# Attention with a gated GLU on one core: the end of the last query chunk rearranged (gate rows kept in SBUF, last division in halves, output weight rows placed anew)

## The chip, the cores and the metric

The kernel runs on 1 core of one Trainium2 chip. The metric is device time in microseconds (us), the median of the runs; lower is better. One more execution was recorded by the hardware profiler; its rows are what is read here. Engines are called PE (matrix unit), PEld (its weight loads), DVE (vector), ACT (scalar), POOL (GpSimd) and SP (the queue that issues nearly all DMAs).

## The reference: what is computed

x is 2048 x 640, there are 32 heads of 20 columns, and the GLU is 1728 wide. Both branches read the same normalised rows.

```python
xn = layernorm(A_x)
q, k, v = split_heads(xn @ wqkv)            # 32 heads of 20
s = softmax(q @ k.T * 20 ** -0.5) @ v       # per head
s = merge_heads(s) @ wo                     # 640 x 640
h = sigmoid(xn @ w_gate) * (xn @ w_up)      # 2048 x 1728
g = silu(h @ w_down)                        # 2048 x 640
out = A_x + s * g
```

## The kernel before, in words

**Tiling.** The heads form 8 groups of 4 (`GH`), the queries 4 chunks of 512 (`QC`), and the keys 16 tiles of 128. A block is one group with one chunk: 32 blocks of 64 jobs, a job being one head against one key tile. The blocks of the last two groups alternate (`gc_of`, line 430), so the last two blocks are group 6 with chunk 3 and group 7 with chunk 3.

**The attention loop.** A job is a score matmul with a contraction of 32 rows (`score_mm`, line 829) into one of two PSUM pairs (`scA`) or one of three single banks (`bk`). ACT takes the exponential of two or three jobs at a time (line 80); DVE computes the exponential of other jobs by bit manipulation: a conversion to `iv` (line 1156) and three passes over four jobs (lines 915, 918, 921). The results, `pt` of ACT and `pb` of DVE, are multiplied with v on PE into the bank `oacc` (`pv_emit`, line 857): 20 rows and a row with the sum for each head.

**The division.** For 31 blocks, `norm_a` and `norm_b` (lines 878 to 908) copy `oacc` to SBUF, send the sums through DRAM and back to invert and broadcast them, multiply on POOL (line 897), and write the result with DMAs (line 905) into `oU`, whose 640 rows lie in 5 tiles of 128 partitions (`KD`). For the very last block the division is a chain of five steps between DVE and PE (`chain`, line 974): copy `oacc` (`e_on`, line 955), four transposes (`e_tr`, line 959), reciprocal and multiply (`div_scale`, lines 709 and 711), four transposes back (`e_back`, line 968), and a copy to a tile of its own, `o7` (`e_o`, line 972).

**The GLU.** Per chunk, gate and up tiles (line 647) give `hT`. Then eight down tiles (`mk_down`, line 677: 14 matmuls into 128 x 320, a tanh on ACT, one DVE operation on line 695) give the rows of g times 4, called `gqs`, which a DMA on SP writes to `gq_dram` (line 697).

**The output.** For chunks 0 to 2, `mk_out` (line 723) multiplies `oU` with `wo`. DVE multiplies with the g rows read back from `gq_dram` (line 742), POOL adds x (line 745), and a DMA stores. For chunk 3 the same is done by hand. `tail_load` (line 929) reads x rows and g rows from DRAM into the room of `wd`. `fill` (line 975) holds 40 matmuls, called fills below: for each of four query tiles, 5 over columns 0 to 511 (into `mains`, lines 940 and 946) and 5 over columns 512 to 639 (into `rest`, 128 wide). They cover the 560 rows that do not come from the last group; the fifth has 48 rows. `late_mm` (line 950) adds the 80 rows of the last group from `o7` with a copy of their weights, `wo_l`: 8 matmuls. `tail_steps` (line 980) ends the kernel: DVE multiplies `rest` (line 988) and adds x (line 993), multiplies each of the four `mains` (line 997), POOL adds x to three of them and DVE to the fourth (line 1000), and four DMAs store (line 1004).

**What sets the order.** PE, ACT and DVE run instructions in the order in which a planner in the kernel emits them (the loop from line 1067). It keeps a clock of its own with assumed durations, and at each step picks for PE a score group, a step of an item (`M`: output, down and other tiles), or a round of the product with v. When it finds nothing to do (`nxt is None`), it emits the next fill, if `can_fill` (line 1042) allows: all jobs claimed, no output or down tile in progress on PE, and for the banks also no items left and the bank free:

```python
if claimed[0] < NJOB * NBLK or cur is not None:
    return False
if f < 0:
    return slots[1]["a"] is None and slots[1]["ends"] <= now
return not items and all(it.bank != f for it in active if it.i < len(it.ops)) and flex[f] <= now
```

The first entry of a fill is `f`: below 0 for the two `mains` in `scA[1]`, 0 and 1 for those in banks 0 and 1, 2 for `rest`. `tail_steps` is emitted when the chain and all fills are out. SP's DMAs stay in the order of emission.

Of the kernel before, what the change touches and what calls it, by code (L numbers as in the profile page):

```python
# [18 lines left out]
P = 128  # L19
# [14 lines left out]

LOG2E = 1.4426950408889634
# [14 lines left out]
def kernel(  # L50
# [625 lines left out]

    def mk_down(c, t4, h, at):
        st = {}
        tt = 4 * c + t4

        def alloc():
            st["ps"] = misc_ps()

        def mm(kf):
            nc.tensor.matmul(st["ps"][:, 0:HD], lhsT=hT[0:fsz[kf], kf, t4 * P:(t4 + 1) * P],  # L685
                             rhs=wd[0:fsz[kf], kf, h * HD:(h + 1) * HD],
                             start=(kf == 0), stop=(kf == NFT - 1))

        def th():
            st["td"] = w2.tile([P, HD], BF16, tag="td", bufs=2, name="td")  # L690
            act_imm(st["td"], st["ps"][:, 0:HD], ACT.Tanh, 0.25)

        def ev():
            gqs = w2.tile([P, HD], FP32, tag="gqs", bufs=3, name="gqs")
            nc.vector.scalar_tensor_tensor(out=gqs, in0=st["td"], scalar=1.0, in1=st["ps"][:, 0:HD],
                                           op0=ALU.add, op1=ALU.mult)
            nc.sync.dma_start(out=gq_dram[tt * P:(tt + 1) * P, h * HD:(h + 1) * HD], in_=gqs)
        return Item([("PE", alloc, [(0.14, lambda kf=kf: mm(kf)) for kf in range(NFT)]),
                     ("ACT", 0.32, th), ("DVE", 0.40, ev, "free", mark("d", c, t4, h))], at, pre=[("h", c, kf) for kf in range(NFT)])


    FL = (NG - 1) * GC
    t_l, o_l = divmod(FL, P)
    wo_l = late.tile([GC, D], BF16, name="wo_l")

    def div_scale(tps):
        tpv = tps.rearrange("p (i j r) -> p i j r", i=4, r=32)
        rq = w2.tile([P, 4, GH, 1], FP32, tag="rt", bufs=2, name="rq")
        nc.vector.reciprocal(out=rq, in_=tpv[:, :, :, 0:1])
        onq = w2.tile([P, 4, GC], BF16, tag="on_bf", bufs=2, name="onq")  # L710
        nc.vector.tensor_tensor(out=onq.rearrange("p i (j e) -> p i j e", e=DH), in0=tpv[:, :, :, 1:1 + DH],
                                in1=rq.broadcast_to((P, 4, GH, DH)), op=ALU.mult)
        return onq
# [173 lines left out]
    def norm_b(b, on, lt):  # L887
# [10 lines left out]
        for j in range(GH):  # L898
            f = g * GC + j * DH
            r = 32 * j + 1  # L900
            left = DH
            while left:
                t, o = divmod(f, P)
                m = min(left, P - o)
                nc.sync.dma_start(out=oU[o:o + m, t, c * QC:(c + 1) * QC], in_=on_bf[r:r + m, :])
                f += m
                r += m
                left -= m
# [15 lines left out]
    wfl = wd.rearrange("p k s -> p (k s)")  # L924
    hfl = hT.rearrange("p k s -> p (k s)")
    EX = D - 512
    tail = []

    def tail_load():
        for t4 in range(4):  # L930
            r = slice(4 * (NQC - 1) * P + t4 * P, 4 * (NQC - 1) * P + (t4 + 1) * P)
            o2 = wfl[:, t4 * 3 * D:(t4 + 1) * 3 * D]
            tail.append((o2[:, 0:D], o2[:, D:3 * D].bitcast(FP32)))
            nc.sync.dma_start(out=tail[t4][0], in_=x2[r, :])
            nc.sync.dma_start(out=tail[t4][1], in_=gq_dram[r, :])


# [6 lines left out]
    def early(dst, t4, sl, kd, start=True):  # L944
        rows = P if kd < t_l else o_l
        nc.tensor.matmul(dst, lhsT=oU[0:rows, kd, c0 + t4 * P:c0 + (t4 + 1) * P], rhs=wo[0:rows, kd, sl],
                         start=(start and kd == 0), stop=False, skip_group_check=True)

    def late_mm(dst, t4, sl):
        nc.tensor.matmul(dst, lhsT=last["o"][:, t4 * P:(t4 + 1) * P], rhs=wo_l[:, sl], start=False, stop=True,  # L950
                         skip_group_check=True)

    def e_on():
        last["on"] = w2.tile([P, QC], FP32, tag="on", bufs=2, name="on")
        nc.vector.tensor_copy(out=last["on"], in_=oacc)

    def e_tr():
        for i in range(4):
            nc.tensor.transpose(out=scA[0][:, 0, i * P:(i + 1) * P], in_=last["on"][:, i * P:(i + 1) * P],
                                identity=ident_f)  # L960

    def e_scale():
        last["q"] = div_scale(scA[0][:, 0, :])

    def e_back():
        last["t"] = psum.tile([P, 2 * QC], BF16, name="tp2", tag="oacc")
        for i in range(4):
            nc.tensor.transpose(out=last["t"][0:GC, i * P:(i + 1) * P], in_=last["q"][:, i, :], identity=ident)

    def e_o():  # L970
        last["o"] = w2.tile([GC, QC], BF16, tag="rl", bufs=1, name="o7")
        nc.vector.tensor_copy(out=last["o"], in_=last["t"][0:GC, 0:QC])

    chain = [("DVE", 0.60, e_on), ("PE", 1.52, e_tr), ("DVE", 0.75, e_scale), ("PE", 0.42, e_back), ("DVE", 0.45, e_o)]
    fill = [(t4 - 2, 0.2133, lambda t4=t4, kd=kd: early(mains[t4], t4, slice(0, 512), kd))
            for t4 in range(4) for kd in range(t_l + 1)]
    fill += [(2, 0.07, lambda t4=t4, kd=kd: early(rest[:, t4 * EX:(t4 + 1) * EX], t4, slice(512, D), kd, t4 == 0))
             for t4 in range(4) for kd in range(t_l + 1)]

    def tail_steps():  # L980
        for t4 in range(4):
            late_mm(rest[:, t4 * EX:(t4 + 1) * EX], t4, slice(512, D))
        for t4 in range(4):
            late_mm(mains[t4], t4, slice(0, 512))
        tmps = [hfl[:, t4 * 2 * D:t4 * 2 * D + 1024].bitcast(FP32) for t4 in range(4)]
        xg = wfl[:, 0:12 * D].rearrange("p (t u) -> p t u", u=3 * D)
        tmp = hfl[:, 8 * D:8 * D + 8 * EX].bitcast(FP32)
        nc.vector.scalar_tensor_tensor(out=tmp.rearrange("p (t e) -> p t e", e=EX),
                                       in0=rest.rearrange("p (t e) -> p t e", e=EX), scalar=0.25,
                                       in1=wfl[:, 0:12 * D].bitcast(FP32).rearrange(  # L990
                                           "p (t u) -> p t u", u=3 * D // 2)[:, :, D // 2 + 512:3 * D // 2],
                                       op0=ALU.mult, op1=ALU.mult)
        nc.vector.tensor_tensor(out=xg[:, :, 512:D], in0=tmp.rearrange("p (t e) -> p t e", e=EX),
                                in1=xg[:, :, 512:D], op=ALU.add)
        for t4 in range(4):
            xr, gqr = tail[t4]
            nc.vector.scalar_tensor_tensor(out=tmps[t4], in0=mains[t4], scalar=0.25, in1=gqr[:, 0:512],
                                           op0=ALU.mult, op1=ALU.mult)
            add = nc.vector if t4 == 3 else nc.gpsimd
            add.tensor_tensor(out=xr[:, 0:512], in0=tmps[t4], in1=xr[:, 0:512], op=ALU.add)  # L1000
        for t4 in range(4):
            r = slice(4 * (NQC - 1) * P + t4 * P, 4 * (NQC - 1) * P + (t4 + 1) * P)
            eng = nc.sync if t4 % 2 == 0 else nc.scalar
            eng.dma_start(out=out2[r, :], in_=tail[t4][0])

    with tc.manual_schedule(engines={ENG.PE, ENG.Activation, ENG.DVE}):
        nc.sync.dma_start(out=wo, in_=A_wo.rearrange("(kd p) e -> p kd e", p=P))
        nc.sync.dma_start(out=wo_l, in_=A_wo[FL:D, :])
# [33 lines left out]
        def can_fill(f):  # L1042
            if claimed[0] < NJOB * NBLK or cur is not None:
                return False
            if f < 0:
                return slots[1]["a"] is None and slots[1]["ends"] <= now
            return not items and all(it.bank != f for it in active if it.i < len(it.ops)) and flex[f] <= now
# [16 lines left out]

        guard = 0
        chain_at = 1e9
        while chain or fill or items or glu_items or any(it.i < len(it.ops) for it in active):
# [11 lines left out]
            if not tail and not glu_items and q_at.get(NBLK - 1, 1e9) <= now and not any(  # L1079
                    it.need is None for it in items + active):  # L1080
# [20 lines left out]
            for eng in ("ACT", "DVE"):  # L1101
                if free[eng] > now:
                    continue
                if chain and chain[0][0] == eng and chain_at <= now:
                    _, dur, f = chain.pop(0)
                    f()
                    free[eng] = now + dur
                    chain_at = now + dur + EL
# [80 lines left out]
            if free["PE"] <= now and chain and chain[0][0] == "PE" and chain_at <= now:  # L1189
                _, dur, f = chain.pop(0)  # L1190
                f()
                free["PE"] = now + dur
                chain_at = now + dur + PL
                mode = "M"
            if free["PE"] <= now:
# [107 lines left out]
                elif nxt is None and fill and can_fill(fill[0][0]):  # L1303
                    free["PE"] = now + fill[0][1] + (T_MODE if mode != "M" else 0.0)
                    fill.pop(0)[2]()
# [47 lines left out]
```

## Time and profile before

| what | value |
|---|---|
| median of 3 runs | 838.99 us (837.27 to 840.88) |
| the profiled execution's own time | 838.14 us |
| its span, first to last instruction | 836.4 us |
| busy: PE, DVE, ACT, POOL | 782.4, 751.7, 798.5, 83.2 us |
| mean granted PE clock | 0.991 |
| PE busy in 807 to 812, and in 812 to 816 | 4.91 of 5.00 us, 3.99 of 4.00 us |
| ACT's last instruction ends | 817.1 us |

How to read it: an instruction row of the timeline gives the start in us from the span's start, the time covered in us, engine, line, operation, output and inputs with shapes, and a count when neighbours are merged; in brackets the idle time before it and what released it. A matmul's row lasts from its start to the end of its result, and the next one starts before that, so the distance between starts is what PE spends on one. The chain of waits gives start, duration and what the time went to, followed back from the last instruction.

### The profile page before, as it was taken

The page shows a single profiled execution, that of the slowest core. Times are in us where ns is not written, and L with a number is a line of the kernel's source. Part 1 is how long each engine was busy: PE and PEld are TensorE (multiplying, and loading weights), DVE is VectorE, ACT ScalarE, POOL GpSimd, SP SyncE. Part 2 cuts the span into 40 slices and gives each one's busy share as a digit, 9 for nine tenths or more (in the row PEclk, how much of TensorE's full clock was granted, in tenths as well). Part 3 has the DMA queues.
Part 4 walks back from the last instruction along what each step waited for, and adds up shares of the span by engine and source line. Part 5 has one row for each costly group of instructions (what it writes and reads, how often), then busy time and mean ns, then how long its engine had stood idle before and what let it go on. Part 6 is the DMA issues. An engine that isn't in the chain of part 4 may idle for free.

```text
span 836.4 us, 16903 instructions
## 1 busy us (share of the span) xinstructions
PE 782.4 (94%) x6330; PEld 276.5 (33%) x6389; DVE 751.7 (90%) x1178; ACT 798.5 (95%) x1000; POOL 83.2 (10%) x90
## 2 busy tenths in 40 slices
PE   4899999999999999999999999999999999999995
PEld 2432223333333323333333323333333223333332
DVE  7689998998899999888999988999889999989994
ACT  7699999999999999999999999999999999999990
POOL 5000000000000000000000000000000003104041
PEclk9899999999999999999999999999999999999998
DMA  5612312122221232212122233221311223314124
GB/s 155 195 31 60 76 43 52 52 61 73 71 68 51 61 85 61 73 50 78 42 62 63 68 84 78 63 83 53 93 46 58 82 81 98 93 46 137 50 72 144
DMA packets 93587, 62.58 MB, mean 75 GB/s; under 512 B 35044, under 2 KB 86884, under 8 KB 93504
## 3 DMA queue, kind: packets, MB, share of 16 engines
q1 hardware_dynamic: 93216, 61.16, 26.0%
q8 instruction: 50, 0.82, 0.4%
q10 hardware_dynamic: 288, 0.33, 0.1%
q14 instruction: 33, 0.27, 0.1%
HBM read 46.51 MB, written 12.40 MB: 70 GB/s over the span
## 4 chain that ended last, share of the span: by engine, by line
ACT 49%; PE 29%; DVE 11%; issue 7%; DMA 2%; SPq 1%; POOLq 0%; POOL 0%; ACTq 0%; DVEq 0%
ACT pt L80 45%; PE scA L830 9%; PE oacc L867 6%; PE bk L685 4%; DVE iv L1156 4%; PE bk L647 4%; ACT tnh L80 2%; DVE pb L921 2%; PE bk L510 2%; DVE pb L915 1%; DVE pb L918 1%; PE bk L735 1%; PE bk L618 1%; PE psk L140 1%; DMA lt<-ld 1%
## 5 line engine op out<-in xcount | busy, mean ns | idle before, releaser
L80 ACT ACTIVATE pt<-scA 128x1024 bf16<-128x1024 f32 x734 | 722.1, 1147 | 5.7 <-PE bk L830 1.9
L1156 DVE TENSOR_SCALAR iv<-bk 128x512 int16<-128x512 f32 x465 | 315.8, 683 | 45.7 <-PE bk L830 44.5
L830 PE MATMUL scA<-q,kT 32*128 32x512 bf16 x1462 | 285.8, 384 | 17.9 <-ACT pt L80 10.5
L830 PE MATMUL bk<-q,kT 32*128 32x512 bf16 x586 | 211.7, 386 | 1.4 <-DVE iv L1156 1.2
L867 PE MATMUL oacc<-pt,v 128*21 128x512 bf16 x1583 | 182.6, 382 | 0.3 <-issue 0.3
L830 PEld LDWEIGHTS <-kT 32*128 32x128 bf16 x2048 | 88.4, 91 | 267.3 <-issue 253.8
L867 PE MATMUL oacc<-pb,v 128*21 128x512 bf16 x930 | 150.6, 382 | 1.0 <-DVE pb L915 0.4
L921 DVE TENSOR_TENSOR pb<-iv,pb 128x2048 bf16<-128x2048 bf16 (+1 forms) x117 | 145.6, 1245 | 0.7
L647 PE MATMUL bk<-xnT,wgu 128*128 128x512 bf16 x475 | 140.5, 383 | 4.6 <-issue 1.9
L897 POOL TENSOR_TENSOR on_bf<-on,rl 128x512 bf16<-128x512 f32 x31 | 42.1, 1358 | 677.4 <-DMA rl<-rd 452.5
L80 ACT ACTIVATE pt<-bk 128x512 bf16<-128x512 f32 x121 | 86.7, 717 | 4.2 <-DVE oacc L388 2.8
L685 PE MATMUL bk<-wd,hT 128*128 128x320 bf16 x448 | 87.1, 302 | 2.2 <-DVE iv L1156 1.5
L915 DVE TENSOR_SCALAR pb<-iv 128x2048 int16<-128x2048 int16 (+1 forms) x117 | 84.5, 722 | 2.7
L918 DVE TENSOR_SCALAR pb<-iv 128x2048 int16<-128x2048 int16 (+1 forms) x117 | 83.4, 713 | 0.0
L867 PEld LDWEIGHTS <-v 128*21 128x21 bf16 x2513 | 49.2, 91 | 85.2 <-issue 62.9
L647 PEld LDWEIGHTS <-wgu 128*128 128x128 bf16 x520 | 37.4, 97 | 65.5 <-issue 47.2
L510 PE MATMUL bk<-xnT,wu 128*120 128x512 bf16 x160 | 50.0, 400 | 0.1
L685 PEld LDWEIGHTS <-hT 128*128 128x128 bf16 x448 | 34.4, 97 | 46.2 <-issue 37.0
L80 ACT ACTIVATE tnh<-bk 128x512 bf16<-128x512 f32 (+1 forms) x56 | 41.5, 742 | 0.1
L655 DVE SCALAR_TENSOR_TENSOR hT<-tnh,bk 128x512 bf16<-128x512 bf16 x52 | 35.3, 680 | 4.3 <-PE bk L647 2.9
L618 PE MATMUL bk<-wv,xnT 128*128 128x160 bf16 x280 | 31.6, 243 | 1.1 <-DVE v L189 0.5
L745 POOL TENSOR_TENSOR xnT<-otmp,xnT 128x320 bf16<-128x320 f32 x24 | 24.2, 1011 | 45.7 <-DVE otmp L742 45.5
(105 smaller groups left out, 366.8 us busy)
## 6 DMA issues: line engine op xcount, KB each, us to landing
rl<-rd SPq DMA_DIRECT2D x124, 64.0 KB
wgu<-in_B_w_gate_dram SPq DMA_DIRECT2D x24, 320.0 KB
wgu<-in_B_w_up_dram SPq DMA_DIRECT2D x24, 320.0 KB
gq_dram<-gqs SPq DMA_DIRECT2D x32, 160.0 KB
xnT<-gq_dram SPq DMA_DIRECT2D x12, 320.0 KB
xt<-in_A_x_dram SPq DMA_DIRECT2D x16, 160.0 KB
oU<-on_bf SPq DMA_DIRECT2D x108, 20.0 KB
wd<-in_B_w_down_dram SPq DMA_DIRECT2D x1, 2080.0 KB
```

Source lines behind the costliest of these rows:

```text
L80: return nc.scalar.add_instruction(mybir.InstActivation(func=func, name=nc.get_next_instruction_name(), engine=ENG.Activation, ins=[nc.sca ...
L510: nc.tensor.matmul(st["ps"][0:UC, :], lhsT=wus[u][:, kd, i, :], rhs=xnT[:, c, kd, :], start=(kd == 0), stop=(kd == KD - 1))
L618: nc.tensor.matmul(st["ps"][:, i * 2 * GC:(i + 1) * 2 * GC], lhsT=xn_tok(tts[i], kd), rhs=wvs[pr][:, kd, :], start=(kd == 0), stop=(kd == ...
L647: nc.tensor.matmul(st[key][0:fs, :], lhsT=w[:, i, kd, ko * P:ko * P + fs], rhs=xnT[:, c, kd, :], start=(kd == 0), stop=(kd == KD - 1))
L685: nc.tensor.matmul(st["ps"][:, 0:HD], lhsT=hT[0:fsz[kf], kf, t4 * P:(t4 + 1) * P], rhs=wd[0:fsz[kf], kf, h * HD:(h + 1) * HD], start=(kf = ...
L830: nc.tensor.matmul(dst, lhsT=kTs[gc_of(b)[0] % 2][32 * j:32 * j + 32, kt * P:(kt + 1) * P], rhs=qts[b % 3][32 * j:32 * j + 32, :], start=T ...
L867: nc.tensor.matmul(oacc[32 * j:32 * j + DH + 1, :], lhsT=lhsT, rhs=u["src"], start=first, stop=last, tile_position=(0, 32 * j), skip_group ...
L897: nc.gpsimd.tensor_tensor(out=on_bf, in0=on, in1=rl, op=ALU.mult)
L915: nc.vector.tensor_scalar(out=pb[:, 0, :, :].bitcast(I16), in0=iv, scalar1=0x7F80, scalar2=1, op0=ALU.bitwise_and, op1=ALU.bitwise_or)
L918: nc.vector.tensor_scalar(out=pb[:, 1, :, :].bitcast(I16), in0=iv, scalar1=0x007F, scalar2=0x3F00, op0=ALU.bitwise_and, op1=ALU.bitwise_or)
L921: nc.vector.tensor_tensor(out=pb[:, 1, :, :], in0=iv.bitcast(BF16), in1=pb[:, 1, :, :], op=ALU.mult)
L1156: nc.vector.tensor_scalar(out=d["iv"][:, j, :], in0=bank[bk], scalar1=B_OFF, scalar2=0.0, op0=ALU.add, op1=ALU.max)
```

## The change: what it does

1. **Gate rows of chunk 3 stay in SBUF.** Line 695's result goes into a tile of the pool `wgu` (`gq_last`, two query tiles each, float32) in place of `gqs`. The 8 writes to `gq_dram` and the 4 reads of chunk 3 are gone. The x rows of chunk 3 are loaded into the room of `xnT`'s chunk 3, as soon as the last `hT` tile of chunk 3 is computed.
2. **Rows of `oU` and `wo` in the last of the five tiles change place.** The last group's 80 rows come first (partitions 0 to 79), the 48 rows before them come after (80 to 127). The fills then run over four full tiles, 32 in place of 40, and each late matmul over the whole fifth tile, 128 rows in place of 80. `wo_l` is gone, and `e_o` writes into `oU`.
3. **The last division runs in two halves of 256 queries.** Each of the five steps becomes two, with dependencies written out; the two scale steps wait for both transposes.
4. **Fills in another order, under another condition.** First the `mains` in banks 0 and 1 (query tiles 2 and 3), then `rest`, then the `mains` in `scA[1]`. Those for banks may start when 24 jobs are unclaimed (`FILL_AT`). A bank with a fill in it is closed to others.
5. **`tail_steps` by halves.** Late matmuls: `mains` 0 and 1, `rest` 0 and 1, then 2 and 3 likewise. DVE: the multiply of `mains` 0 and 1, then `rest` of these two (256 wide), the same for 2 and 3, and the addition for `mains` 3 at the end.

The diff, cut to its core:

```diff
+FILL_AT = 24
+    def gq_last(t4):
+        if len(gq_l) == t4 // 2:
+            w = w2.tile([P, 2, KD, 2 * P], BF16, tag="wgu", bufs=2, name="gql")
+            gq_l.append(w.rearrange("p i k f -> p (i k f)").bitcast(FP32))
+        return gq_l[t4 // 2][:, t4 % 2 * D:(t4 % 2 + 1) * D]
...
         def ev():
+            if c == NQC - 1:
+                nc.vector.scalar_tensor_tensor(out=gq_last(t4)[:, h * HD:(h + 1) * HD], in0=st["td"], scalar=1.0,
+                                               in1=st["ps"][:, 0:HD], op0=ALU.add, op1=ALU.mult)
+                return
...
+                if t == KD - 1:
+                    o = f - FL if f >= FL else f - FK + D - FL
                 nc.sync.dma_start(out=oU[o:o + m, t, c * QC:(c + 1) * QC], in_=on_bf[r:r + m, :])
...
-            nc.sync.dma_start(out=tail[t4][0], in_=x2[r, :])
-            nc.sync.dma_start(out=tail[t4][1], in_=gq_dram[r, :])
+            tail.append(xl[:, t4 * D:(t4 + 1) * D])
+            nc.sync.dma_start(out=tail[t4], in_=x2[r, :])
...
-        nc.tensor.matmul(dst, lhsT=last["o"][:, t4 * P:(t4 + 1) * P], rhs=wo_l[:, sl], start=False, stop=True,
-                         skip_group_check=True)
+        nc.tensor.matmul(dst, lhsT=oU[:, KD - 1, c0 + t4 * P:c0 + (t4 + 1) * P], rhs=wo[:, KD - 1, sl], start=False,
+                         stop=True, skip_group_check=True)
...
-    chain = [("DVE", 0.60, e_on), ("PE", 1.52, e_tr), ("DVE", 0.75, e_scale), ("PE", 0.42, e_back), ("DVE", 0.45, e_o)]
+    chain = [("DVE", 0.34, lambda: e_on(0), ()), ("DVE", 0.34, lambda: e_on(1), ()),
+             ("PE", 0.40, lambda: e_tr(0), (0,)), ("PE", 0.40, lambda: e_tr(1), (1,)),
+             ("DVE", 0.50, lambda: e_scale(0), (2, 3)), ("DVE", 0.50, lambda: e_scale(1), (2, 3)),
+             ("PE", 0.25, lambda: e_back(0), (4,)), ("PE", 0.25, lambda: e_back(1), (4, 5)),
+             ("DVE", 0.27, lambda: e_o(0), (6,)), ("DVE", 0.27, lambda: e_o(1), (7,))]
...
-            for t4 in range(4) for kd in range(t_l + 1)]
+            for t4 in (2, 3, 0, 1) for kd in range(KD - 1)]
+    fill[2 * (KD - 1):2 * (KD - 1)] = [
+        (2, 0.07, lambda t4=t4, kd=kd: early(rest[:, t4 * EX:(t4 + 1) * EX], t4, slice(512, D), kd, t4 == 0))
+        for t4 in range(4) for kd in range(KD - 1)]
...
+        for i in range(2):
+            for t4 in (2 * i, 2 * i + 1):
+                late_mm(mains[t4], t4, slice(0, 512))
+            for t4 in (2 * i, 2 * i + 1):
+                late_mm(rest[:, t4 * EX:(t4 + 1) * EX], t4, slice(512, D))
+        for i in range(2):
+            for t4 in (2 * i, 2 * i + 1):
+                nc.vector.scalar_tensor_tensor(out=tmps[t4], in0=mains[t4], scalar=0.25, in1=gq_last(t4)[:, 0:512],
+                                               op0=ALU.mult, op1=ALU.mult)
+                if t4 < 3:
+                    nc.gpsimd.tensor_tensor(out=tail[t4][:, 0:512], in0=tmps[t4], in1=tail[t4][:, 0:512], op=ALU.add)
+            nc.vector.scalar_tensor_tensor(out=tmp[:, 2 * i:2 * i + 2, :],
...
+            nc.vector.tensor_tensor(out=xg[:, 2 * i:2 * i + 2, 512:D], in0=tmp[:, 2 * i:2 * i + 2, :],
+                                    in1=xg[:, 2 * i:2 * i + 2, 512:D], op=ALU.add)
+        nc.vector.tensor_tensor(out=tail[3][:, 0:512], in0=tmps[3], in1=tail[3][:, 0:512], op=ALU.add)
...
+        nc.sync.dma_start(out=wo[:, 0:KD - 1, :], in_=A_wo[0:FK, :].rearrange("(kd p) e -> p kd e", p=P))
+        nc.sync.dma_start(out=wo[0:GC, KD - 1, :], in_=A_wo[FL:D, :])
+        nc.sync.dma_start(out=wo[GC:P, KD - 1, :], in_=A_wo[FK:FL, :])
...
         def can_fill(f):
-            if claimed[0] < NJOB * NBLK or cur is not None:
+            if cur is not None or NJOB * NBLK - claimed[0] > (FILL_AT if f >= 0 else 0):
                 return False
             if f < 0:
                 return slots[1]["a"] is None and slots[1]["ends"] <= now
+            if f in filled:
+                return True
...
-            if not tail and not glu_items and q_at.get(NBLK - 1, 1e9) <= now and not any(
-                    it.need is None for it in items + active):
+            if not tail and all(ev_at.get(("h", NQC - 1, kf), 1e9) <= now for kf in range(NFT)):
                 tail_load()
...
                 elif nxt is None and fill and can_fill(fill[0][0]):
                     free["PE"] = now + fill[0][1] + (T_MODE if mode != "M" else 0.0)
+                    if fill[0][0] >= 0:
+                        filled.add(fill[0][0])
+                        flex[fill[0][0]] = 1e9
                     fill.pop(0)[2]()
```

## The prediction

> **What bounds the kernel now.** I read the page first. ACT, PE and DVE are all near full until the last slice, so no stage before the end has spare time, and the change touches only the end.
>
> ```profile
> PE   4899999999999999999999999999999999999995
> DVE  7689998998899999888999988999889999989994
> ACT  7699999999999999999999999999999999999990
> ```
>
> Then the chain of waits over the last 17 us, which says what the end hangs on:
>
> ```profile
> 818.29 1.19 PE scA L946 x4
> ...
> 820.11 4.44 DMA gq_dram<-gqs
> ...
> 824.62 2.72 DMA wd<-gq_dram
> ...
> 827.41 0.70 DVE hT L988
> ...
> 831.97 1.56 POOLq L1348
> ```
>
> The last gate tile goes to DRAM (4.44 us) and comes back (2.72 us); only then, at 827.41, does DVE start the tail. That looks like 7 us to be had. The chain names only the last arrival, though, so I looked at what came just before it, in PE's timeline:
>
> ```profile
> 817.37 0.59 PE L946 MATMUL scA<-wo,oU 128*128 128x512 bf16 x2 [0.16 <-issue]
> 817.90 0.39 PE L867 MATMUL oacc<-pt,v 128*21 128x512 bf16 x1
> ...
> 818.22 1.25 PE L946 MATMUL scA<-wo,oU 128*128 128x512 bf16 x4
> 819.40 0.39 PE L867 MATMUL oacc<-pb,v 128*21 128x512 bf16 x1
> 819.72 0.93 PE L946 MATMUL scA<-wo,oU 128*128 128x512 bf16 x3
> ...
> 822.74 0.39 PE L968 MATMUL tp<-ident,onq 128*80 128x128 bf16 x4
> 822.96 2.87 PE L946 MATMUL bk<-wo,oU 128*128 128x512 bf16 x23
> 825.76 0.40 PE L950 MATMUL bk<-wo_l,o 80*128 80x128 bf16 x4
> 826.00 0.59 PE L950 MATMUL scA<-wo_l,o 80*128 80x512 bf16 x2
> 826.43 0.59 PE L950 MATMUL bk<-wo_l,o 80*128 80x512 bf16 x2
> ```
>
> PE works on fills (L946) without a gap until 825.76, and its late matmuls end at 827.02, only 0.39 us before DVE starts. The division's last copy ended at 823.64, so neither the division nor the DMA holds PE: the fills do. The DMA pair hides a PE queue nearly as long as itself. Last, DVE and POOL:
>
> ```profile
> 817.20 0.49 DVE L695 SCALAR_TENSOR_TENSOR gqs<-td,bk 128x320 f32<-128x320 bf16 x1 [0.56 <-ACT td L80]
> 828.14 0.69 DVE L993 TENSOR_TENSOR wd<-hT,wd 128x512 bf16<-128x512 f32 x1
> 829.71 3.83 POOL L1000 TENSOR_TENSOR wd<-hT,wd 128x512 bf16<-128x512 f32 x3 [16.48 <-DVE hT L997]
> 831.46 1.07 DVE L1000 TENSOR_TENSOR wd<-hT,wd 128x512 bf16<-128x512 f32 x1
> ```
>
> POOL's third addition ends at 833.54; its store and the closing take 2.86 us more, to 836.4. I keep these 2.86 us: the last store remains one of the same size.
>
> **The change, step by step.** All times are of the profiled execution.
>
> *Early fills (FILL_AT): 0.* A fill needs an empty list of items and no tile in progress on PE. The last output tile starts at 809.05, and from there PE goes from row to row (3.99 of 4.00 us busy from 812 to 816) until the last down tile ends at 815.78, after all scores are out. There is no idle step for the planner to give away, so I expect the order up to 817 unchanged. The bounds are below, as rivals.
>
> *Fills before the last v product: 0.45 us gained.* Before, seven fills stand ahead of it (one record of them is missing). Following the planner's rules, the last down tile lies in bank 0, and now the first fill is for bank 0, so it waits until line 695 has read that bank: 817.69, some 0.09 later on PE. That is a new wait; behind it in PE's queue stand the other fills and the last v product. The three fills of 817.1 to 817.9 fall out, the pair of v products moves ahead of them, and I count five fills before the last product becomes ready for the planner: 817.78 + 5 x 0.213 (819.72 to 820.57 is four) = 818.85, and with the 0.1 that a switch costs (818.22 to 819.40 holds four fills and more) the product starts at 818.95 in place of 819.40. It can't start before 818.03, when `pb` is done.
>
> *PE from there to the late matmuls: 6.04 becomes 5.2 us.* Before, from 819.72 to 825.76: 13 fills of 512 columns x 0.213 = 2.77, 20 narrow ones at 0.108 (822.96 to 825.76 less 3 x 0.213, over 20) = 2.16, the transposes 0.65 (820.59 to 821.24) and 0.22, idle 0.24. After: 32 fills less 5 leave 11 x 0.213 = 2.35 and 16 x 0.108 = 1.73; the transposes keep 0.87; for two more handovers between DVE and PE I add 0.25. So from 819.27 to 824.47.
>
> *The halves of the division: hidden.* Half a copy of `oacc` has no row; it lies between 0.34 (half of 0.69) and 0.69. From 0.49 for 320 columns and 0.69 for 512 I take 0.42. Then 819.37 + 2 x 0.42 = 820.21 for the copies, 820.9 for the second transposes, two scale halves of 0.6 each (0.26 and 0.49 halved in their variable part) 822.0, back and copied by 823.0. PE has fills to 824.47, so the division is covered by 1.5 us; without that cover its own length would count.
>
> *DVE's start: 2.46 us earlier.* Now wide late matmuls come first. First result 0.39 after its start and 0.09 for switch and semaphore: 824.95 in place of 827.41.
>
> *DVE's tail: 0.5 us shorter.* Before, 6.13 us from 827.41 to POOL's end. After, DVE does four multiplies of 0.65 (828.94 to 830.24 for two) = 2.60, two half multiplies of 0.42 = 0.84, two half additions, and one addition of 512. An addition of this form took 0.69 alone (L993) and 1.07 beside POOL (L1000), a factor of 1.55. The halves run beside POOL: 2 x 0.42 x 1.55 = 1.30 (bounds 0.84 and, each waiting for a whole POOL addition of 1.28, 3.4). The last runs as POOL ends: 0.69. Gaps 0.2. Sum 5.63. POOL, fed from 0.65 on, needs 3.83 and ends at about 4.6, ahead of DVE. So the end is 824.95 + 5.63 + 2.86 = 833.44 in place of 836.4: 2.96 us gained.
>
> The Trainium skill's "SBUF — State Buffer", section "Who interferes with whom", says that a DVE operation with two SBUF inputs and a GpSimd operation that reads SBUF share a port as an exclusive lock, the later one blocked for the whole instruction. The row differs: 1.07 us beside POOL is 0.38 more than alone, far less than the 0.8 then left of POOL's addition (its second ended near 832.26). By the rule the two half additions would lose some 0.5 us more, and the end would be 833.9.
>
> *At nothing:* the gate result written into SBUF under another name (0.49 either way; the `wgu` buffers had their last reader before the last `hT` row at 733.43, so there is no wait); one more weight DMA at the start, hidden behind 800 us of other work (bounds 0 and 0.7, an issue of line 905); eight writes and four reads less on SP, which in the last 40 us waited mostly for POOL and DVE. The x loads now fall to about 734.1, right behind that `hT` row: four issues of 0.37 on SP, and behind them the inverted sums of a division, sent at 735.15 before. They may go 0.5 later; POOL waits for them for microseconds anyway, and only an output tile much later reads the result (bounds 0 and 0.9).
>
> *Sum:* -2.96. The profiled execution took 838.14, so 835.2; the median of the runs lies 0.85 above it, and I put the forecast on the median: 838.99 - 2.96 = **836.0**, that is 0.35% faster. A measurement of this kernel can tell about 0.5%, or 4.2 us, from no change, so the likeliest reading is "the same".
>
> **Rivals.**
>
> *Forecast (0.66): PE's fills stay the last to arrive.* Own range -2.2 to -3.8: port bounds of DVE's additions (-0.5 to +0.8) and 0.3 either way on PE; 834.9 to 836.8 before scatter.
>
> *Fills really go early (0.13).* If the planner finds idle steps for some 15 fills before the last product, PE is done when the division is. The product then starts at 818.1, 0.85 sooner; the division takes 3.65 from there on (823.0 less 819.37), so late matmuls start near 822.2 in place of 824.47. That is 2.3 more: -5.2, 833.8. For it: the division had been ready 2.1 us before PE. Against: PE shows no gap to put them in.
>
> *The split costs PE what the fewer fills save (0.13).* A handover from DVE to PE showed 0.29 (820.51 to 820.80) and 0.5 (822.22 to 822.74). If each of the four new ones stops PE by that because no fill is placed between, PE loses 1.2 to 2.0 in place of 0.25; the DMA's removal then uncovers PE at once and gains little: -1.3 to -2.0, about 837.3. For it: PE's order is fixed by assumed durations.
>
> *Slower (0.08): the early fill blocks PE.* One of bank 0's four fills reads the tile of `oU` that the second of five DMAs of line 905 completes. Those start at 812.51, 0.7 apart; issue to use took 1.67 beyond the last issue for line 895's, so that tile is there at 815.5. Should the four come out right after 809.05's tile, PE stands from about 810.9 to 815.5: 4.6 us in which DVE and ACT run dry, with 1 us to refill. -2.96 + 5.6 = +2.6: 841.6. It decides against the change from a stall of 3 us on, and as measurably slower from 7 us. For it: nothing in the condition looks at that DMA. Against: the same lack of idle steps.
>
> **How the numbers follow.** The three runs spread over 3.6 us, so a difference of medians carries about 1.5 us. Of the forecast's 0.66 some 0.13 then falls beyond -4.2, with most of 0.13 from early fills: faster 0.25. Slower by over 4.2: 0.03. Within: 0.72. The range takes in the forecast with its scatter, the third case, and the near part of the second: 833.9 to 838.3.
>
> **What would show it.** Right: the chain's end without a DMA link before DVE; PE's fills up to about 824.5 and DVE's first multiply near 825.0; PE's rows before 817 in the same order; five fills before the last v product; the last addition on DVE near 830.5. Wrong: fills before 815; idle time of PE between 819 and 824.5; DVE's start before 824 or after 826; half additions of over 0.9 us.

## The result

| | before | changed |
|---|---|---|
| median | 838.99 us (836.02 to 842.81, 7 runs) | 832.09 us (831.65 to 834.81, 7 runs) |
| profiled execution, span | 836.4 us | 829.9 us |
| mean granted PE clock in it | 0.991 | 0.997 |
| the last score group (line 830, now 842): start of its third matmul | 814.51 | 811.98 |
| from there to the end of the span | 21.91 us | 17.92 us |

The ratio is 0.9926, interval 0.9898 to 0.9953: faster by 6.9 us, where 3.0 were forecast. Twelve later runs gave a ratio of 0.995 (0.9924 to 0.9975): 833.54 against 837.6, 4.1 us. The last two rows of the table say why the two differ: 3.99 us of the 6.5 us between the profiles lie at the end, where the change is, and 2.5 us were there before the first instruction that it moves.

The page of the changed kernel, by slices, is that of before to within a tenth up to the last slice:

```profile
PE   4799999999999999999999999999999999999996
...
DVE  7789998998899999888999988999989998989996
ACT  7799999999999999999999999999999999999992
...
PEclk9999999999999999999999999999999999999998
```

In the last slice PE has 6 where it had 5, DVE 6 for 4 and ACT 2 for 0. The row of the clock has a 9 in its second place, where before had an 8: a small digit, to which experiment 6 comes back.

Its chain of waits no longer holds a DMA. It runs over PE's fills (now line 955), the transposes of the division, and DVE:

```profile
816.38 0.32 PE oacc L879
816.70 0.75 PE bk L955 x3
...
818.27 0.34 DVE onq L723
...
819.54 1.73 PE scA L955 x8
821.26 0.45 PE scA L959 x2
821.71 0.02 issue
821.73 1.29 DVE hT L1018 x2
```

PE's timeline, to be compared with the one in the prediction (its times lie about 2.5 us lower throughout):

```profile
815.14 1.24 PE L955 MATMUL bk<-wo,oU 128*128 128x512 bf16 x5 [0.24 <-DVE gql L704]
816.31 0.39 PE L879 MATMUL oacc<-pb,v 128*21 128x512 bf16 x1
816.63 0.82 PE L955 MATMUL bk<-wo,oU 128*128 128x512 bf16 x3
...
817.82 0.78 PE L955 MATMUL bk<-wo,oU 128*128 128x128 bf16 x11
818.65 0.31 PE L980 MATMUL tp<-ident,onq 128*80 128x128 bf16 x2
...
821.10 0.59 PE L959 MATMUL scA<-wo,oU 128*128 128x512 bf16 x2
```

Five fills stand ahead of the last v product, as forecast, and the first waits for line 704 (695 before). But eleven narrow fills take 0.62 us, counted from start to start (817.82 to 818.44, 0.056 each), not the 1.19 that 0.108 each would make; and the late matmuls come 4.47 us after the fill that follows that product (816.63 to 821.10), not 5.2. DVE and POOL:

```profile
821.73 1.29 DVE L1018 SCALAR_TENSOR_TENSOR hT<-scA,gql 128x512 f32<-128x512 f32 x2 [1.98 <-PE scA L959]
...
823.39 0.61 DVE L1026 TENSOR_TENSOR xnT<-hT,xnT 128x256 bf16<-128x256 f32 x1
...
825.57 0.84 DVE L1026 TENSOR_TENSOR xnT<-hT,xnT 128x256 bf16<-128x256 f32 x1
826.33 0.68 DVE L1028 TENSOR_TENSOR xnT<-hT,xnT 128x512 bf16<-128x512 f32 x1
822.57 3.56 POOL L1021 TENSOR_TENSOR xnT<-hT,xnT 128x512 bf16<-128x512 f32 x3 [11.89 <-DVE hT L1018]
```

DVE ends last, at 827.01, and 2.89 us later the span ends: the 2.86 of before.

### The profile page after: what moved, and what is told of

It reads as the page before. It is cut to its first block, busy times and chain, and to the rows that moved or that the text cites. A ratio compares the mean times of both kernels' runs of the same rounds, so it can differ in the third digit from the quotient of the medians.

```text
span 829.9 us, 16926 instructions
## 1 busy us (share of the span) xinstructions
PE 785.7 (95%) x6381; PEld 274.5 (33%) x6381; DVE 752.2 (91%) x1184; ACT 798.1 (96%) x1000; POOL 82.9 (10%) x90
## 5 line engine op out<-in xcount | busy, mean ns | idle before, releaser
L648 PE MATMUL bk<-xnT,wgu 128*128 128x512 bf16 x520 | 149.3, 383 | 2.6 <-DVE iv L1185 1.2
L694 PEld LDWEIGHTS <-hT 128*128 128x128 bf16 x448 | 34.4, 97 | 45.2 <-issue 35.9
L81 ACT ACTIVATE tnh<-bk 128x512 bf16<-128x512 f32 (+1 forms) x56 | 40.9, 731 | 0.1
```

Source lines behind the costliest of these rows:

```text
L81: return nc.scalar.add_instruction(mybir.InstActivation(func=func, name=nc.get_next_instruction_name(), engine=ENG.Activation, ins=[nc.sca ...
L648: nc.tensor.matmul(st[key][0:fs, :], lhsT=w[:, i, kd, ko * P:ko * P + fs], rhs=xnT[:, c, kd, :], start=(kd == 0), stop=(kd == KD - 1))
```

## The experiments

Because 2.5 us came from elsewhere, each kernel is read twice: its median beside the kernel before on the same chip, and, in its profile, the time from the last score group to the end of the span, called its **end** here and counted from the start of that group's third matmul. The end is steady: 17.92, 17.85, 17.88 and 17.91 us in four executions of the changed end. (Counted from the group's first matmul, a_order has 17.39 in place of 17.20; elsewhere the two differ by 0.06 at most.)

| kernel | median (before, same chip) | ratio, interval | end |
|---|---|---|---|
| before | 837.6 to 838.2 on three chips | | 21.91 |
| gate rows only (e_gate) | 835.37 (837.9) | 0.9976, 0.9957 to 0.9995 | 20.65 |
| rows placed only (e_rows) | 838.65 (837.9) | 0.9998, 0.9979 to 1.0018 | 22.68 |
| both of these (e_both) | 833.04 (837.6) | 0.9944, 0.9923 to 0.9965 | 17.80 |
| both, new tail order (e_mix) | 833.42 (837.6) | 0.9956, 0.9936 to 0.9975 | 17.32 |
| whole change (after_again) | 833.54 (837.6) | 0.995, 0.9924 to 0.9975 | 17.85 |
| change, old fill order (a_order) | 832.22 (837.79) | 0.9941, 0.9918 to 0.9963 | 17.20 |
| change, 48-row fills (a_rows48) | 835.54 (837.9) | 0.9968, 0.995 to 0.9986 | 20.34 |
| the same, filled up to 128 (a_rows128) | 833.9 (837.9) | 0.9951, 0.9936 to 0.9967 | 18.77 |

**1. Gate rows alone.** Edit: the new branch in `ev` of `mk_down`, `gq_last`, and `tail_load` with x only; all else as before.

> The kernel before with the gate rows of the last chunk kept in SBUF and nothing else changed (the narrow multiply of the tail in two pieces, since the rows lie in two tiles). Theory A (PE's queue of fills ends only 0.4 us before the DMA pair it was hidden behind): DVE's tail starts when the first late matmuls are done, 1.2 us sooner than before; the time falls by 1.0 to 1.5 us, 0.15%. Rival B (the DMA pair was the bound): it falls by 4 us or more, most of what the whole change brings at its end.

The end fell by 1.26 us, as A says, with the DMA pair gone entirely. (The median fell by 2.5 us, more than forecast; the interval of its ratio leaves room for 0.4 to 3.6.) Its chain of waits shows what stood behind the pair:

```profile
821.65 2.70 PE bk L957 x23
824.35 0.34 PE bk L961 x4
824.70 0.02 issue
824.72 0.77 DVE hT L1000 x2
```

PE's fills run straight up to the late matmuls, and DVE starts as the first of these end. Rival B is ruled out.

**2. Rows placed alone.** Edit: the new offset in `norm_b`, the split load of `wo`, fills over four full tiles, late matmuls over the fifth.

> The kernel before with the rows of oU and wo placed anew and nothing else: 32 fills over full tiles, late matmuls over 128 rows; the gate rows still go through DRAM. Theory A: PE's late matmuls start 2 us or more sooner, but DVE still waits for the DMA pair at the same place; time unchanged within 0.5 us. Rival B: PE's saving shows in the time, 2 us or more faster.

Late matmuls started 8.50 us after the last score group in place of 11.25, and none of it reached the time. The chain:

```profile
819.77 5.05 DMA gq_dram<-gqs
...
824.90 2.81 DMA wd<-gq_dram
...
827.88 0.70 DVE hT L986
```

DVE waits for the DMA pair as before; this time the write took 5.05 us where the profiled execution of before had 4.44, and the end is 0.8 later for that. So each of the two parts hides the other.

**3. Both together.**

> The kernel before with parts 1 and 2 only (gate rows in SBUF, rows placed anew); division in one piece, fills in the old order and under the old condition, old order of the tail. From the profiles of the two single steps: the first late matmul 8.5 us after the last score group (with the rows alone), 0.43 to DVE's start, 8.96 from there to the end (with the gate rows alone): 17.9 us, as much as the whole change has (17.92). Theory G (the two parts bring all of it together, and neither alone, since each uncovers the other): the same time as the changed kernel within 0.5 us. Rival H (the halves and the new order carry a good part): 1 us or more slower than the changed kernel.

> Parts 1, 2 and 5: as the kernel with parts 1 and 2, with the changed kernel's order of the tail by halves (wide late matmuls first). Theory G: first late matmul at 8.5 us after the last score group, DVE 0.63 later, 8.17 from there to the end as in the changed kernel: 17.3 us, 0.6 us faster than the changed kernel. Rival H: the division in halves is needed for the early start; 17.9 us or more.

Theory G holds for the end: 17.80 with the two parts, 17.32 with the new order of the tail as well, so the changed kernel's other parts (halves, order of fills) cost about 0.6 us. The median with the new order shows no gain over the whole change (833.42 and 833.54, where 0.6 was expected); eleven of its twelve runs had a mean clock of 0.994 or less, a matter of experiment 6.

**4. Which of them costs it.** Edit: `for t4 in range(4)` in `fill`, the narrow ones at the end, as before; halves kept.

> The changed kernel with the old order of the fills (those into the pair scA first, then banks 0 and 1, the narrow ones last); division in halves as in the changed kernel. Theory I (the new order makes PE wait 0.42 us for line 704 to read bank 0, and puts the cheap narrow fills under the division, so PE also waits 0.36 us there): the first late matmul comes 8.5 to 8.7 us after the last score group in place of 9.1, the time is 0.5 us shorter. Rival J (the order is right, the halves cost it): 9.1 or later.

The first late matmul came at 8.42 us, the end at 17.20. It is the order, not the halves: the changed kernel's PE waits 0.42 us for bank 0 (814.72 to 815.14; some 0.1 of it any switch from a v product to a fill costs, see experiment 5) and twice, 0.21 and 0.16 us, under the division, where now only narrow fills lie. FILL_AT costs and brings nothing: with 0 in place of 24 the planner emits the same program.

**5. The 48 rows.**

```diff
-        nc.tensor.matmul(dst, lhsT=oU[:, kd, c0 + t4 * P:c0 + (t4 + 1) * P], rhs=wo[:, kd, sl],
+        rows = P if kd < t_l else o_l      # a_rows128: rows = P, and zeros written into these rows of oU
+        nc.tensor.matmul(dst, lhsT=oU[0:rows, kd, c0 + t4 * P:c0 + (t4 + 1) * P], rhs=wo[0:rows, kd, sl],
```

> The changed kernel with its second part undone: 40 fills, eight of them with 48 rows, and late matmuls with 80 rows from a tile of their own. Theory C (a matmul whose rows differ from those of its neighbour cannot have its weights loaded under that neighbour, so a 48-row fill costs 0.43 wide and 0.26 narrow, with both switches): DVE's start is 2.5 to 2.9 us later after the last v product than in the changed kernel, and the time is 2.5 to 2.9 us longer. Rival D (the prediction's mean prices of 0.213 and 0.108 for a fill of any height): 1.3 us longer.

> As the changed kernel with its second part undone, but each fifth fill runs over all 128 rows; the 80 rows that do not belong to it are zeros in oU, written once at the start, so the sum is the same. As many matmuls as with 48 rows, no change of height among the fills, one before the late matmuls. Theory C: eight fills of full height cost 4 x 0.216 + 4 x 0.056 = 1.1 us; the time lies 1.0 to 1.3 us above the changed kernel and 1.5 us below the kernel with 48 rows. Rival D: the same time as with 48 rows.

Against 17.92 the ends are +2.42 and +0.85: the same number of fills, 1.57 us apart (1.64 between the medians, on one chip). Of the 1.57, 1.29 lie ahead of DVE's first multiply (11.98 and 10.69 us after the last score group); the rest came in the tail, where the two programs are alike, and is taken for scatter. The ends lie 0.1 to 0.2 us under what theory C expects; its figure for DVE's start after the last v product was 2.5 to 2.9 us later with 48 rows, and 2.1 was measured. Rival D falls: it expects no difference between the two. The weight loads by shape show the mechanism; the columns are busy time and mean, then idle time ahead of them. First with 48 rows, then with 128:

```profile
L955 PEld LDWEIGHTS <-oU 128*128 128x128 bf16 x32 | 2.3, 97 | 2.4 <-issue 1.3
L955 PEld LDWEIGHTS <-oU 48*128 48x128 bf16 x8 | 0.7, 92 | 2.0 <-issue 1.6
```

```profile
L955 PEld LDWEIGHTS <-oU 128*128 128x128 bf16 x40 | 3.1, 98 | 2.5 <-issue 0.9
```

A 48-row load has 0.25 us of idle time ahead of it (2.0 over 8), one of 128 rows among its like 0.06 (2.5 over 40). A load of 128 rows behind one of 128 starts under the matmul ahead of it. One of 48 rows does not, nor does the load of 128 rows behind it, and each time about 0.1 us is lost: wide fills then start 0.31 and 0.32 us after the one ahead in place of 0.216, narrow ones 0.15 and 0.16 in place of 0.056. The rows were there in the profile of before, and I had not read them:

```profile
L946 PEld LDWEIGHTS <-oU 128*128 128x128 bf16 x32 | 2.1, 97 | 2.0 <-issue 1.6
L946 PEld LDWEIGHTS <-oU 48*128 48x128 bf16 x8 | 0.7, 92 | 1.9 <-issue 1.5
```

Theory C blames any difference of rows between neighbours, and that is too wide. In a_rows128 the late loads of 80 rows follow fills of 128 without a wait:

```profile
821.98 0.31 PEld L955 LDWEIGHTS <-oU 128*128 128x128 bf16 x2
822.41 0.86 PEld L959 LDWEIGHTS <-o 80*128 80x128 bf16 x6
```

The first of the six starts with the last fill, and its matmul comes 0.216 us after that fill. On the other hand a v product, whose weights have 128 rows but 21 columns, costs the same 0.1 us on the way in and on the way out (816.00, 816.31 and 816.63 in the changed kernel). So the price of 48 rows among 128 is shown; which shapes pay it, and why, is open. The Trainium skill's "TensorE: Matmul & The Clock Gate", section "LDWEIGHTS (loading the stationary operand)", says that a load's time goes by columns, not by rows. The durations agree (92 and 97 ns); the wait ahead of it is not in that rule.

**6. The 2.5 us that are not at the end.** The granted clock in the stretch after 33 us, of before and then of the changed kernel (the stretch and its length, then PE, PEld, DVE, ACT, POOL busy, clock, DMA share and GB/s):

```profile
33.40:40.20 6.80, 6.22 (x41) 3.36 (x42) 3.39 (x7) 4.65 (x6) 0.00 (x0) 0.50 1.09 347
```

```profile
33.40:40.20 6.80, 5.66 (x61) 3.39 (x58) 5.42 (x10) 6.68 (x9) 0.00 (x0) 1.00 1.08 348
```

For 6.8 us PE ran at half clock, 41 matmuls in place of 61, with the same order of work in both. What it cost is read from ACT's first and seventh exponential of the attention loop, of before and then of the changed kernel:

```profile
34.36 0.60 ACT L80 ACTIVATE pt<-bk 128x512 bf16<-128x512 f32 x1 [2.79 <-DVE oacc L388]
...
40.52 3.77 ACT L80 ACTIVATE pt<-scA 128x1024 bf16<-128x1024 f32 x4
```

```profile
33.52 0.60 ACT L81 ACTIVATE pt<-bk 128x512 bf16<-128x512 f32 x1 [2.57 <-DMA wgu<-in_B_w_gate_dram]
...
38.10 3.83 ACT L81 ACTIVATE pt<-scA 128x1024 bf16<-128x1024 f32 x4
```

The distance between the kernels grows from 0.84 to 2.42 us: the stretch costs 1.58, and 0.84 were there before it. Of these, 0.25 are PE's pace at its start: fifteen transposes (line 278, now 279) took 1.33 us from 19.09 in the one profile and 1.08 from 18.71 in the other; in both they start 0.107 us apart at first and 0.056 at the end, and the pace changes at 19.7 in the one and at 18.8 in the other. That point too differs between executions of one kernel: 19.0 and 20.7 us in the two profiles of before with the filling below (b_warm, b_warm2), with the first exponential at 33.52 and 34.58. Nor does the distance stay at 2.42: at the 101st exponential it is 1.50 (127.39 and 125.89), at the 601st 1.64, and it comes back to 2.5 only between 767 and 796 us. That it ends near its value behind the stretch is in part chance.

PE has idle time just before, 1.30 and 0.79 us ahead of lines 174 and 830, so I filled it (`warm(n)` issues n matmuls of 512 columns into a free bank, their result unused; its definition is left out here):

```diff
         def s_bound(eng):
+            warm(5)
             q_bound(pq[0], 0, pq[1])
+            warm(3)
```

> The changed kernel once more, to have it beside the others on one chip. Theory E (part of the measured 6.9 us is a matter of single executions: stretches of 6.83 us at half the granted clock, which the kernel before showed at 33.4 us in its profiled execution): against the kernel before it is 4.0 us, 0.48%, faster among runs of equal mean clock, and the median difference lies between 3.5 and 6 us, with some runs near 830.0 us of span and others 2.5 us above. Rival F (the change itself removes those stretches): nearly all runs have a mean clock of 0.997 and a span near 830, as in the first seven.

> The changed kernel with eight matmuls more whose result is not used (512 columns each, into a bank that is free), five ahead of the matmul that waits near 31 us and three behind it, where PE is idle for 2 us before the attention loop. Theory W (the stretch of half clock near 33 us follows from PE's idle time in the stretch before): every run has a mean clock of 0.995 or more, the spread shrinks to 1 us, and the median is 1 to 2 us below the changed kernel's on the same chip. Rival: the mean clocks scatter as without, and the time is the same or up to 0.3 us longer.

> The kernel before with the same eight unused matmuls in PE's idle time near 31 us, and nothing else. Theory W: the mean clock is 0.995 or more in nearly all runs, where most runs of the kernel before are at 0.987 to 0.994, and the median falls by 2 to 3.5 us against before. With the clock even, the difference to the changed kernel with the same matmuls (829.7) is the change alone: 4.0 us by the profiles' tails (21.9 against 17.9 after the last score group). Rival: the clock scatters as before, no gain.

> The kernel before with eight unused matmuls near 31 us, again, now beside the changed kernel with the same matmuls on one chip. With the half-clock stretch at 33 us gone from both, theory A and C (the end is worth 4.0 to 4.7 us by the profiles) expect 4.0 to 4.7 us between the two medians. A change of the clock's behaviour by the change itself would show as 6 us or more.

> The changed kernel with the same eight matmuls: 4.0 to 4.7 us below the one named before, on the same chip; 2 to 3.5 us below the changed kernel without them, most runs with a mean clock of 0.995 or more.

The changed kernel went from 833.54 to 829.71 us beside it (six runs at a mean clock of 0.997 or 0.998, where the twelve without ranged from 0.986 to 0.998), and to 829.38 on another chip (829.24 to 830.09). The kernel before went from 837.79 to 835.41 and from 838.2 to 834.90. Theory W holds in its direction; its sizes were off (in a_warm 3.8 us gained, not 1 to 2, and a spread of 3.0 us, not 1; in b_warm nine of twelve runs at a mean clock of 0.995 or more). E holds, F falls: the same changed kernel had the stretch in one profiled execution (after_again, 34.1 to 40.9) and not in another.

What decides it within one execution is not shown. In the 6.8 us ahead of the stretch near 33 us PE was busy for 3.46 us (e_both), 3.64 (e_mix), 4.06 to 4.07 (after_again, a_order, e_rows) and 4.19 (before), and with the filling for 5.74 to 5.88, where the clock did not fall. That looks like a threshold, but the changed kernel's first profile had 4.07 us of work from 26.6 to 33.4 and 4.05 from 29.1 to 35.9 and kept its clock, and in a_order the clock fell at two later places as well, after much more work:

```profile
207.90:214.70 6.80, 5.50 (x44) 1.69 (x44) 6.21 (x10) 6.75 (x10) 0.00 (x0) 1.00 0.11 28
214.80:218.10 3.30, 3.30 (x25) 1.03 (x18) 1.28 (x2) 2.47 (x4) 0.00 (x0) 0.50 0.68 195
566.30:573.10 6.80, 5.94 (x61) 2.67 (x57) 6.80 (x10) 6.80 (x9) 1.27 (x1) 1.00 0.46 134
573.20:576.50 3.30, 3.30 (x24) 1.10 (x17) 3.30 (x6) 2.14 (x3) 0.00 (x0) 0.50 0.10 26
```

The Trainium skill's "TensorE: Matmul & The Clock Gate", section "Part 1: The HAM clock gate (the "warmup" mystery)", says that the window in which PE's activity is judged runs freely, 3.4 us long, and that an idle window halves the clock. The lengths agree: stretches of 3.4 (e_both), 6.8 and 10.2 us (e_mix). But PE was not idle for a whole window here: in the 3.4 us ahead of the stretch of before it worked for 1.50.

Nor is the stretch near 33 us all that the filling removes. The first profile of the changed kernel had none, and its last score group came at 811.98; with the filling it came at 809.27 (a_warm) and 809.65 (a_warm2). What the other 2.3 to 2.7 us are was not followed up.

Between the two kernels with filling on one chip lie 5.5 us (4.0 to 4.7 were expected), and 4.5 us between the ends in their profiles (22.43 and 17.91; the DMA pair took 4.83 + 2.84 this time). The other 1.0 us is not settled. In the two profiles the last score group came at 812.47 and 809.65, and 1.5 us of that were there at the first exponential (34.58 and 33.09); but in another execution of the former (b_warm) it came at 809.55. Whether the change itself shifts how often the clock falls was not told apart either.

**7. A faster version.**

> Parts 1, 2 and 5 (as the kernel that had 17.3 us after its last score group), with the eight unused matmuls near 31 us, and sixteen more at the start, on zeros, before the first transpose near 10 us. Theory W: PE is then at full clock from its first transposes, where it ran them at half; the first stage gets 1 to 2 us shorter; with 0.5 us from the tail the median is 1.5 to 2.5 us below the changed kernel with eight matmuls (829.7), near 828. Rival: the first stage is bound by loads, DVE and ACT, and only the 0.5 us of the tail show: 829.2.

> The same, with the products of the tail kept in bfloat16 in place of float32, so DVE's three additions read 16-bit operands alone. From a 16-bit multiply of 2048 columns in 1.22 us (0.60 ns a column) against 0.69 us for 512 columns with a float32 operand: the last addition takes 0.35 in place of 0.69, the half additions 0.2 to 0.4 in place of 0.61 and 0.84; the end comes 0.7 to 1.0 us sooner. If they wait for POOL's port instead, no gain.

> The changed kernel with the old order of the fills, products of the tail in bfloat16, and the eight matmuls near 31 us: 16.7 us after the last score group (17.2 with the old order, less 0.5 for bfloat16), so 1.2 us below the changed kernel with eight matmuls on the same chip, and below both kernels by 4 and 8 us.

The sixteen matmuls at the start brought nothing: 832.45 us (ratio 0.9929, 0.9908 to 0.995), where the changed kernel with eight near 31 us had 829.71 and 829.38 on other chips; theory W expected 828, the rival 829.2. The clock rose at 4.5 us (matmuls of 512 columns 0.427 us apart before, 0.216 after) and fell at 11.4; in between PE waited from 6.5 to 10.25 for the first rows. The stretch of half clock now lay in the first stage, and one more of 3.4 us came at 212.7:

```profile
4.60:11.30 6.70, 2.92 (x24) 1.51 (x22) 6.53 (x19) 5.22 (x14) 3.33 (x5) 1.00 0.90 253
11.40:18.10 6.70, 4.97 (x20) 2.20 (x20) 5.32 (x12) 6.04 (x16) 4.95 (x12) 0.50 0.46 115
```

With bfloat16 products as well: 831.16 (0.9922, 0.9901 to 0.9943), end 16.81 in place of 17.32. Those products are rounded to 16 bits before x is added. DVE's last rows in c_best:

```profile
822.79 0.70 DVE L1033 TENSOR_TENSOR xnT<-hT,xnT 128x256 bf16<-128x256 bf16 x1
823.42 0.41 DVE L1035 TENSOR_TENSOR xnT<-hT,xnT 128x512 bf16<-128x512 bf16 x1
```

The last addition took 0.41 in place of 0.68, the half beside POOL 0.70 in place of 0.84: the gain of 0.5 us is less than forecast, since this half took 0.70 where 0.2 to 0.4 was expected. That POOL is what keeps it slow is likely but not shown apart. c_best (old fill order, 16-bit products, filling at 31 us only) had 828.84 us against 829.38 for the changed kernel with filling, both against 838.2 (ratios 0.9892, 0.9871 to 0.9913, and 0.9897, 0.9877 to 0.9917); its end was 16.89. That is below both kernels, but the step to the changed kernel with filling is smaller than the 1.2 us expected and lies inside the intervals.

## Why the prediction was wrong, point by point

- **What bounds the end: right.** PE's fills, not the DMA pair, stood behind everything; with the pair removed alone, 1.26 us came out (experiment 1). The 7 us that the chain of waits seems to offer were never there.
- **Early fills: right.** The order up to the first fill is unchanged and FILL_AT without effect. With that the rivals "fills really go early" and "slower, the early fill blocks PE" fell: the first fill came at 815.14, which is 817.67 on the time axis of the profile before.
- **Fills before the last v product: right.** Five; the product started 4.34 us after the last score group in place of 4.89, 0.55 sooner where 0.45 was forecast.
- **PE from there to the late matmuls: the step that failed.** It was to go from 6.04 to 5.2 us and went to 4.47. I took 0.108 us as the price of a narrow fill, a mean over 16 of full height and 4 of 48 rows. The full ones cost 0.056; each of 48 rows costs 0.2 more for the two switches, wide or narrow. What the change takes out is exactly the dear ones: by a_rows48, eight fills with their switches are worth 2.4 us. The 4.47 are 11 x 0.216 + 16 x 0.056 + 0.81 for the transposes + 0.37 of idle time.
- **The halves of the division: nearly right.** They were to be hidden by 1.5 us; with the narrow fills at 0.056 the cover grew thin and PE waited 0.37 us, one of the prediction's own signs of being wrong. The rival "the split costs PE what the fewer fills save" has this loss, but at 1.2 to 2.0 us.
- **DVE's start:** 3.15 us sooner after the last score group (12.90 to 9.75), forecast 2.46; the difference is the step above (0.73), with 0.1 more from the v product and 0.15 less from DVE's start behind the first late matmul.
- **DVE's tail: mis-sized by 0.35.** 5.28 us in place of 5.63. The half additions took 0.61 and 0.84, 1.45 together against 1.30 forecast, but multiplies and additions follow each other without the gaps that I added, and the second half addition's row overlaps the next one. By the lock that the prediction quotes from the Trainium skill's "SBUF — State Buffer", section "Who interferes with whom", it would have been longer still. Measured, DVE beside POOL pays a part of POOL's instruction, not all: 0.61 and 0.84 us beside additions of 1.2 on POOL.
- **From the profiled execution to the median: the larger failure.** The forecast took 836.4 us as the kernel's own and its scatter as noise. It held 2.5 us ahead of the change that the profile of the changed kernel did not: a stretch of half clock worth 1.6 us where it lies, written in the row of slices for PE's clock and in its mean of 0.991, 0.84 us lost before it, and what came and went between there and the end. Of the seven runs of the changed kernel four had a mean clock of 0.997 or more and took 831.65 to 832.09 us; the other three, at 0.991 to 0.993, took 832.23 to 834.81. The end alone would have given 838.99 - 3.99 = 835.0, inside the range; the measured 832.09 lies outside by what differed ahead of the end. Part of that is the luck of the executions, as the 4.1 us of the later runs show: 838.99 less 4.1 would have been inside. The mis-sized fill would have been wrong all the same.

## What to carry to other kernels

A wait that ends last hides the queue just behind it: look up when the next engine was free, and expect only the difference; two parts that alone bring 1.3 us and nothing may bring 4.1 together. When matmuls are priced, take the spacing of each shape and the idle time ahead of its weight loads, not a mean over a row that merges them. Before a span is used as a base, look at the granted clock by stretches: a gap of PE that is cheap to fill with unused matmuls was worth as much here as most of the change.

## What was not expected of the hardware

- Weight loads of 48 rows between loads of 128 did not start under the matmul ahead of them, nor did the load behind them: about 0.1 us for each switch, 1.3 us ahead of DVE's start for eight fills (a_rows48 against a_rows128). Loads of 80 rows behind one of 128 paid nothing.
- The clock fell to half for 3.4, 6.8 or 10.2 us without a long idle time of PE. PE's work in the 6.8 us ahead was 3.46 to 4.19 us in six profiles, near 33 us, but 5.50 and 5.94 us at two later places of a_order, and 4.05 us in the changed kernel without a fall. Filling 2 us near 31 us was worth 3.8 us in the median of the changed kernel and 2.4 and 3.3 us in the kernel before.
- PE began at half pace, and when it reached the full one differed between executions of one kernel: 19.0 and 20.7 us (b_warm, b_warm2).
- The write of 160 KB to DRAM and the dependent read took 6.8 to 7.9 us in four executions with the same pair of DMAs (3.86 + 2.90, 4.44 + 2.72, 4.83 + 2.84, 5.05 + 2.81).
